# A linear-attention and gated-MLP kernel: chunks 0 and 1 get a triangular solve of their own, and the solve of chunks 2 and 3 goes to GpSimd

## The chip, the core and the metric

The kernel runs on one core of a Trainium2 chip. The core has five engines that run their own instruction lists in order and wait for each other by semaphores: TensorE (PE), VectorE (DVE), ScalarE (ACT), GpSimd (POOL) and SyncE (SP), which here issues the DMA transfers. The metric is the device time of one execution in microseconds, here the median of three runs.

## What is computed

A delta-rule attention over 768 steps for 4 x 8 heads of width 48, and on its output a gated MLP of 3072 tokens, 384 by 1536:

```python
k_n = k / (np.linalg.norm(k, axis=-1, keepdims=True) + 1e-06)
for t in range(S):
    y[:, :, t] = np.einsum('bhd,bhde->bhe', q[:, :, t], state)
    v_old = np.einsum('bhde,bhd->bhe', state, kt)
    state = state + bt[:, :, :, None] * np.einsum('bhd,bhe->bhde', kt, vt - v_old)
x = attn_out.transpose(0, 2, 1, 3).reshape(B * S, H * D)
a = x @ w_a
b = x @ w_b
return (a * b @ w_out)
```

## The kernel before

The 768 steps are cut into 24 chunks of 32. Within a chunk the recurrence is a unit triangular system per head: its 32 x 32 matrix comes from products of keys (the "G" products, TensorE, from the loaded tile `rawb` into a PSUM bank or `duo`), is scaled by VectorE into `b_0`, transposed into `b_1`, and inverted by forward substitution. Chunks go in groups of four (`GROUPS`); one group's 4 x 32 heads fill the 128 partitions, so a group is solved at once. `prep(g)` loads keys, norms and scaling factors and forms the matrices, `solve(g)` inverts, `steps(g)` runs the chunks: state read ("K"), correction ("U"), output ("A"), state update ("S").

The first group is solved in halves (`HALVES`): two 16 x 16 blocks are inverted by 30 dependent VectorE instructions (15 multiplies into `tmp`, 15 subtractions from `b_2`), and `join` builds the missing block on TensorE: the "W" products (64x16 for chunks 0 and 1, 32x16 for 2 and 3), a ScalarE copy `wr`, then the "X" products with the transposed inverse `b_3` and with `xn`. Chunks 0 and 1 use masked, doubled operands (`kk2`, `cx`, `at2`, `tt2`, all lying in the weight tile `wt`), so that a chunk is 16 products of 64x48 instead of 32.

The expert weights come as 12 blocks of 1.15 MB. VectorE decodes each by a TENSOR_SCALAR and two SCALAR_TENSOR_TENSOR instructions over 128x1152 integers. For the first two pairs of chunks the MLP runs in float32 (per block six products with `xb` of 256 columns, a ScalarE copy `a`, a VectorE product `g`, two products of 384 columns), later with float16 parts.

Nothing of the order is written out: every call is put down as an `Op` of the planner class `Plan`, with a price (`price`), the ops it depends on and, for TensorE, a due time (`slot`, `when`). `pack` plays the engines forward and at each step gives a free engine its most urgent ready op; the resulting lists are what the chip runs. While TensorE would idle before 40 us of the plan, `pack` puts in fillers: products of constants into a spare bank (`wide`, `ones`), so that the clock stays up. The plan is made before anything runs: if an engine is slower on the chip than its price, the order stays and the others wait.

Loads are issued by SP in the order of `EARLY`; some are held behind a tiny copy that GpSimd makes once an earlier tile is there:

```python
if over and what != "s" and len(over) < THROTTLE:
    dst = goal(c, what)
    G.tensor_copy(dst, over[max(0, len(over) - 2)])
```

Each such 1x1 copy waits for the load before last and writes into the next load's target, which makes that load wait in turn. The first of them follow chunk 1's correction `u`.

Of the kernel before, what the change touches and what calls it, by code (L numbers as in the profile page):

```python
# [12 lines left out]
F32 = mybir.dt.float32  # L13
# [13 lines left out]
P = 128  # L27
KR = 112
GROUPS = [list(range(i, i + 4)) for i in range(0, NCH, 4)]
# [3 lines left out]
HALVES = [1, 0, 0, 0, 0, 0]  # L33
# [16 lines left out]
def slot(c, piece):  # L50
    if piece == "G" and c < 4:
        v = -30 + 0.1 * c
# [17 lines left out]
EARLY = [(0, "k"), (0, "b"), (2, "k"), (0, "r"), (2, "r")], [(0, "m"), (0, "v"), (2, "v"), (0, "w"), (1, "w")], [(2, "w")], [(3, "w"), (4, "w"), (4, "k"), (4, "r"), (5, "w")], [(6, "w"), (6, "k"), (6, "r"), (7, "w"), (4, "v"), (6, "v"), (8, "w")]  # L70
LAG = 2
THROTTLE = 18
PADS, WARM = 40, 4
# [11 lines left out]
class Plan:  # L85
# [93 lines left out]
    def price(eng, name, outs, ins, kw):  # L179
# [27 lines left out]
        if eng == "DVE":  # L207
# [15 lines left out]
            return (66 + n / speed) / 0.96 + extra  # L223
        return 40 + n / 1.2

    def add(self, eng, fn, name, args, kw):
# [20 lines left out]
        else:  # L247
# [4 lines left out]
            if eng == "PE":  # L252
                op.use += dur
# [46 lines left out]
    def stall(self, o, t, pos, edge, come, then):  # L300
# [3 lines left out]
        while end > edge - self.AHEAD:  # L304
            if then is None:
                enter = max(t + halt + max(0, edge - self.AHEAD - pos) * each, come)
                busy = max(0.0, min(self.BUSY, self.dma - enter - 1000.0)) if enter < 110e3 else 0.0
# [6 lines left out]
        return halt, end, edge, come, then  # L314

    def pack(self, pri, back=False):
# [9 lines left out]
        until, use, warm = self.OPEN, 0.0, True  # L326
# [8 lines left out]
        while len(done) < n:  # L335
# [66 lines left out]
            if e == "PE" and not back:  # L402

                if kept and t > self.SINCE:
# [4 lines left out]
                    def spend(f, many, words, brief):  # L409
                        nonlocal until, warm, use, pos, edge, come, then  # L410
                        while True:
                            while until <= f:
                                warm = use > 0.43 * self.WINDOW if warm else use > 0.75 * self.WINDOW
                                use, until = 0.0, until + self.WINDOW
                            idle.words, idle.dur = words, brief if warm or wide else 2 * brief
# [4 lines left out]
                            use, f = use + idle.dur, f + step[0] + idle.dur  # L420
                            pos, edge, come, then = step[1:]

                    if wide:
                        kept_ = until, warm, use, pos, edge, come, then
                        many = spend(f, 0, 4, 871.0)
                        until, warm, use, pos, edge, come, then = kept_
                        burn = max(0, (edge - self.PEEK - pos - 4 * many) // 4)
                        if burn < 40:
# [5 lines left out]
                        many = spend(f, 0, 4, 871.0)  # L434
                        fine = int((stop_ - f - 871.0 * many) // 218.0)
                        pos += 2 * fine
                    else:
                        many, fine = 0, spend(f, 0, 2, 218.0)
                    fill[i] = burn, many, fine
                while until <= t:  # L440
                    warm = use > 0.43 * self.WINDOW if warm else use > 0.75 * self.WINDOW
                    use, until = 0.0, until + self.WINDOW
# [3 lines left out]
                full = took * o.use / o.dur  # L446
                part = min(1.0, (until - t) / took)
                use += full * part
                if part < 1.0:
                    warm = use > 0.43 * self.WINDOW if warm else use > 0.75 * self.WINDOW  # L450
                    use, until = full * (1 - part), until + self.WINDOW
# [28 lines left out]
    BLOCK, EDGE, FETCH, BUSY, FIRST, AHEAD, STALL, PEEK = 256, 193, 4100.0, 2500.0, 1000.0, 30, 250.0, 2  # L480
# [5 lines left out]
    WINDOW, OPEN = 3413.0, 9800.0  # L486
# [62 lines left out]
def tile_kernel(ctx, tc, kqt, kqs, kn, vn, beta, w, masks, picks, out):  # L549
# [234 lines left out]
    dcs = {}  # L784
    nmr = ring(cst, "nm", 3, [P, 32], F32)
# [9 lines left out]
    tmpt = one("tmp", [P, 256])  # L795
# [60 lines left out]
    def prep(g):  # L856
        chs = GROUPS[g]
        ss = sst
        for c in chs[::2]:
            if g > 1:  # L860
                load(c, "t")
# [6 lines left out]
        s0, s1 = s0t, s1t  # L868
        dc = dcs[g] = dcr()
        nm = nmr()  # L870
# [8 lines left out]
        V.tensor_mul(dc, s0, bt[:, g * 32 : g * 32 + 32])  # L879
# [4 lines left out]
        for ci, c in enumerate(chs[::2] if g > 1 else ()):  # L884
# [28 lines left out]
        for ci, c in enumerate(() if g > 1 else chs):  # L913
            rw = raw(c)
            ga = (duo[:, ci % 2] if g or ci < 1 else att()).rearrange("p (q n) -> p q n", n=64)
            plan.behind = set(ready + hold if g else ())
# [11 lines left out]
            if c == 2:  # L928
                gate.append(len(plan.ops) - 1)
            V.tensor_mul(  # L930
                gnat.rearrange("p k u -> p u k")[:, ci * 8 : ci * 8 + 8, :],
                ga[:, :, 0:32],
# [7 lines left out]
            elif HALVES[g]:  # L940
                kks[c] = ttr()
                plan.behind = {said}
                A.copy(kks[c], ga[:, :, 0:32])
            if ci % 2 == 0:
                at = atr()
            if c < 2:
# [6 lines left out]
                )  # L953
                yield
                continue
            ats[c] = at[:, ci % 2]
            if g < 1:
                plan.behind = {said}
                A.copy(ats[c], ga[:, :, 32:64])
            V.tensor_mul(ats[c], ats[c] if g < 1 else ga[:, :, 32:64], amask.unsqueeze(1).broadcast_to([P, 8, 32]))  # L960
            if c == 3:
                gx = att().rearrange("p (q n) -> p q n", n=64)
                plan.due = slot(c, "G") + 20e3
                with plan.group():
                    for q, h4, a, _ in heads():
                        T.matmul(
                            gx[tok(h4), q, :],
                            raw(0)[feat(h4), a, h4 % 2],
                            raw(1)[feat(h4), a],
                            start=True,  # L970
                            stop=True,
                            skip_group_check=True,
                        )
                for x, h4 in product(range(2), range(4)):
                    o = 32 * ((h4 + x) % 2)
                    A.copy(cx[x][tok(h4), :, o : o + 32], gx[tok(h4), :, o : o + 32])
# [3 lines left out]
        for ci, c in enumerate(chs):  # L980
            (V if g < 1 else G).tensor_mul(
# [6 lines left out]
    def solve(g):  # L988
# [8 lines left out]
        V.tensor_copy(X.rearrange("p t s -> p (t s)")[:, 0 : 33 * 31 + 1 : 33], dtt)  # L997
        size = 16 if HALVES[g] else 32
# [7 lines left out]
        for k in range(size - 1):  # L1006
            m, w = size - 1 - k, k + 1
            tv = tmpt[:, 0 : nb * m * w].rearrange("p (b m w) -> p b m w", b=nb, w=w)
# [368 lines left out]
    st = [lab(f"steps{g}", steps(g, GROUPS[g] if g else [0, 1])) for g in range(NG)]  # L1377
    rest = lab("rest", steps(0, GROUPS[0][2:]))

    plan.stream = "load"  # L1380
    for n, part in enumerate(EARLY[:3]):
        if n == 1:
            G.tensor_copy(mk[0:1, 0:1], rawp(2)[0:1, 0, 0:1])
        if n == 2:
            G.tensor_copy(place(2)[0:1, 0:1], place(0)[0:1, 0:1])
# [11 lines left out]
    for c, what in EARLY[3]:  # L1397
        load(c, what)
# [15 lines left out]
    def opening():  # L1414
# [4 lines left out]
        for c, what in EARLY[4]:  # L1419
            load(c, what)  # L1420
        plan.stream = "rest"
        yield next(pr[1])
        for n in range(2):
            for _ in range(3):
                yield next(rest)
            yield next(pr[1])
            yield next(pr[1])
        yield from chain([rest, pr[1]])
# [9 lines left out]
    merge((moes, 15), (sv[1], 8))  # L1438
# [94 lines left out]
```

## Time and profile before

| | before |
|---|---|
| median of 3 runs (lowest to highest) | 613.67 us (612.68 to 613.83) |
| profiled execution | 613.47 us |
| its span, first to last instruction | 611.7 us |
| PE busy | 601.5 us, 98% |
| DVE busy | 404.1 us, 66% |
| ACT busy | 301.5 us, 49% |
| POOL busy | 34.8 us, 6% |
| mean granted TensorE clock | 0.989 |

Busy time of PE is modelled up to the end of a product's pipeline and includes the fillers; the list of waits tells better where it stood still. In rows of a timeline, several like instructions are merged (x32), and a float32 product leaves two records. The bracket at the end of a row is the idle time of that engine just before it and what ended it.

### The profile page before, as it was taken

Reading aid. Unit: us, or ns where it says so; the run is one execution under the profiler, and the core shown is the slowest. Engines: PE = TensorE matmul, PEld = TensorE weight load, DVE = VectorE, ACT = ScalarE, POOL = GpSimd, SP = SyncE. Lnnn points to the kernel's source line nnn. Section 1 sums busy time; section 2 is a strip of 40 time slices with the busy share of each in tenths; the row PEclk is TensorE's granted clock in tenths of the full one; section 3 lists DMA queues with packets and bytes.
Section 4 is the critical chain, followed back from the end, with each engine's and each line's share of the span. In section 5 each row is a group of like instructions: output and inputs, shape, how many; then the busy total and the mean of one; then the engine's idle time right before and its main releaser. Section 6 shows DMA issues by size and latency. Waiting matters only on the chain.

```text
span 611.7 us, 25252 instructions
## 1 busy us (share of the span) xinstructions
PE 601.5 (98%) x11469; PEld 470.4 (77%) x11469; DVE 404.1 (66%) x1093; ACT 301.5 (49%) x756; POOL 34.8 (6%) x49
## 2 busy tenths in 40 slices
PE   8999999999999999999999999999999999999997
PEld 5588766787778787887787788787777788777875
DVE  5849878897799845699653996553996344244222
ACT  4312313589745753554655366445356445535322
POOL 1000240001100010000101000101000000000000
PEclk9969999999999999999999999999999999999999
DMA  6718688101311204104013013010000000000000
GB/s 221 269 55 318 240 318 301 54 0 32 124 42 48 94 4 153 59 15 135 4 59 122 4 36 115 3 37 20 3 28 3 3 28 2 3 27 3 27 1 26
DMA packets 11931, 46.46 MB, mean 76 GB/s; under 512 B 1328, under 2 KB 4784, under 8 KB 8752
## 3 DMA queue, kind: packets, MB, share of 16 engines
q1 hardware_dynamic: 11824, 44.85, 20.9%
q8 instruction: 89, 1.46, 1.0%
q14 instruction: 18, 0.15, 0.1%
HBM read 40.13 MB, written 4.72 MB: 73 GB/s over the span
## 4 chain that ended last, share of the span: by engine, by line
PE 70%; DVE 5%; ACT 2%; issue 0%
PE bank L545 58%; PE duo L545 9%; PE S_ps L545 2%; DVE b L545 1%; DVE tmp L545 1%; ACT y L545 1%; DVE g L545 1%; DVE wt L545 0%; DVE ghl L545 0%; ACT sqf L545 0%; ACT a L545 0%; DVE at L545 0%; ACT wt L545 0%; DVE f L545 0%; ACT tt L545 0%
## 5 line engine op out<-in xcount | busy, mean ns | idle before, releaser
L545 PE MATMUL bank<-xb,wt 128*128 128x256 f16 (+1 forms) x1800 | 248.5, 291 | 2.4 <-issue 2.4
L545 PEld LDWEIGHTS <-wt 128*128 128x128 f16 x2160 | 208.2, 98 | 35.4 <-issue 0.5
L545 DVE TENSOR_TENSOR g<-bank,a 128x256 f32<-128x256 f32 x144 | 60.4, 419 | 123.4 <-ACT a L545 121.9
L545 PE MATMUL bank<-wt,ghl 128*128 128x384 f16 x720 | 137.1, 326 | 0.0
L545 ACT ACTIVATE a<-bank,gs 128x256 f32<-128x256 f32 x120 | 56.8, 473 | 121.8 <-PE bank L545 121.5
L545 PEld LDWEIGHTS <-ghl 128*128 128x128 f16 x720 | 67.5, 98 | 34.4
L545 PE MATMUL bank<-stage,wt 128*128 128x256 f16 x648 | 76.9, 273 | 0.0
L545 ACT CAST ghl<-g 128x256 f16<-128x256 f32 x120 | 48.4, 403 | 52.1 <-DVE g L545 51.8
L545 DVE TENSOR_TENSOR ghl<-g,ghl 128x256 f16<-128x256 f32 x120 | 51.0, 425 | 34.2 <-ACT ghl L545 33.7
L545 PEld LDWEIGHTS bank<-xb,wt 128*128 128x128 f32 x288 | 53.3, 190 | 14.3 <-issue 3.4
L545 DVE TENSOR_TENSOR b<-b,tmp 128x31 f32<-128x31 f32 (+20 forms) x170 | 56.6, 333 | 3.7
L545 DVE TENSOR_TENSOR tmp<-b,b 128x31 f32<-128x31 f32 (+20 forms) x170 | 56.3, 331 | 3.6
L545 ACT COPY y<-duo 32x384 f32<-32x384 f32 x88 | 41.4, 470 | 3.3 <-PE duo L545 2.2
L545 PE MATMUL bank<-wt,g 128*128 128x384 f32 x96 | 37.3, 500 | 0.0
L545 POOL TENSOR_TENSOR vnb<-vnb,nm 128x384 f32<-128x384 f32 x20 | 18.0, 921 | 128.0 <-DMA vnb<-in_vn 70.2
L545 DVE TENSOR_TENSOR f<-vnb,duo 128x768 f32<-128x768 f32 (+1 forms) x23 | 21.4, 929 | 5.4 <-issue 4.3
L545 ACT COPY a<-bank 128x256 f32<-128x256 f32 x24 | 8.8, 367 | 29.5 <-PE bank L545 29.4
L545 ACT COPY u<-duo 128x768 f32<-128x768 f32 (+1 forms) x23 | 18.0, 784 | 10.2 <-PE duo L545 9.9
L545 ACT ACTIVATE sqy<-y 128x96 f32<-128x96 f32 x80 | 22.3, 278 | 0.9
L545 PEld LDWEIGHTS duo<-sh,rawb 48*64 48x64 f32 x1152 | 18.4, 134 | 4.7 <-issue 2.9
L545 PEld LDWEIGHTS duo<-f,tt 32*32 32x32 f32 x1408 | 16.5, 105 | 6.9 <-issue 4.3
L545 PEld LDWEIGHTS bank<-wt,g 128*128 128x128 f32 x96 | 17.1, 189 | 6.0
(156 smaller groups left out, 624.7 us busy)
## 6 DMA issues: line engine op xcount, KB each, us to landing
rawb<-in_kqt SPq DMA_DIRECT2D x10, 1024.0 KB, 5.0
stage<-in_w SPq DMA_DIRECT2D x6, 1152.0 KB, 6.7
vnb<-in_vn SPq DMA_DIRECT2D x12, 384.0 KB, 4.5
out<-ob SPq DMA_DIRECT2D x24, 192.0 KB, 1.9
knb<-in_kn SPq DMA_DIRECT2D x10, 384.0 KB, 3.5
stage<-in_kqs SPq DMA_DIRECT2D x8, 448.0 KB, 3.9
late<-in_w SPq DMA_DIRECT2D x3, 1152.0 KB, 7.4
wt<-in_w SPq DMA_DIRECT2D x3, 1152.0 KB, 8.4
```

The lines of the kernel that those rows point to most:

```text
L545: fn(*(self.place(a, lease) for a in args), **{k: self.place(a, lease) for k, a in kw.items()})
```

## The change

`GROUPS` becomes [0, 1], [2, 3] and then fours. The first solve therefore has only chunks 0 and 1; it runs the same 30 instructions, with half the partitions unused (zeroed at the start by GpSimd). Its preparation needs one `knb` and one `rawb` load, and the load list puts the second pair's loads behind these. Chunks 2 and 3 become group 1: their G products are made early and copied to SBUF by ScalarE, their scaling and transposition are VectorE's, and their 30 solve instructions are GpSimd's (`E = G if g == 1`), with a `tmp` half of their own. The scaling of V for chunks 0 and 1 moves from two VectorE instructions to 16 ScalarE instructions. Weight blocks 1 and 2 are each held by a 1x1 GpSimd copy behind the solutions `tt2` of chunk 0 and of chunk 1. In the planner, TensorE's activity is kept as a sum of weighted columns, fillers are added where the sum would fall under `NEED`, the price of a GpSimd tensor instruction is 120 + 4.0 n, and the 40 tiny products at the start go. The core of the diff:

```diff
-GROUPS = [list(range(i, i + 4)) for i in range(0, NCH, 4)]
+GROUPS = [[0, 1], [2, 3]] + [list(range(i, i + 4)) for i in range(4, NCH, 4)]
-HALVES = [1, 0, 0, 0, 0, 0]
+HALVES = [int(c[0] < 4) for c in GROUPS]
...
-        v = -30 + 0.1 * c
+        v = -30 + 0.1 * c if c < 2 else -10 + 0.1 * c
...
-        v = 5.0 + 2.2 * (c - 4) if c < 8 else finish(c // 4 * 4 - 4 + c % 4 // 2) - 0.5 + 0.1 * (c % 2)
+        v = 6.5 + 2.2 * (c - 4) if c < 8 else finish(c // 4 * 4 - 4 + c % 4 // 2) - 0.5 + 0.1 * (c % 2)
...
-EARLY = [(0, "k"), (0, "b"), (2, "k"), (0, "r"), (2, "r")], [(0, "m"), (0, "v"), (2, "v"), (0, "w"), (1, "w")], [(2, "w")], ...
+EARLY = [(0, "k"), (0, "b"), (0, "r"), (2, "k"), (2, "r")], [(0, "m"), (0, "v"), (2, "v"), (0, "w")], ...
+SHARE, QUOTA = {32: 0.24, 48: 0.19, 64: 0.5}, 1515.0
-PADS, WARM = 40, 4
+PADS, WARM = 0, 4
...
+        if name.startswith("tensor_") and n > 1:
+            return 120 + 4.0 * n
         return 40 + n / 1.2
...
+                    while t > self.SINCE + self.WINDOW and self.worth(spent, t + o.dur) + o.use < self.NEED:
+                        idle.words, idle.dur = 2, 218.0
+                        halt, pos, edge, come, then = self.stall(idle, t, pos, edge, come, then)
+                        spent.append((t + halt, 218.0, 0.159))
+                        t, fine = t + halt + 218.0, fine + 1
...
-            if c == 2:
-                gate.append(len(plan.ops) - 1)
+            if 1 < c < 4:
+                kks[c] = ttr()
+                A.copy(kks[c], ga[:, :, 0:32])
...
-            (V if g < 1 else G).tensor_mul(
+            if c < 2:
+                for q in range(8):
+                    x = vnc(c)[:, q * D : q * D + D]
+                    A.activation(x, x, AF.Copy, scale=nm[:, ci * 8 + q : ci * 8 + q + 1])
+                continue
+            (V if c < 4 else G).tensor_mul(
...
+        E = G if g == 1 else V
...
-            V.tensor_mul(tv, lk.unsqueeze(3).broadcast_to([P, nb, m, w]), xk.broadcast_to([P, nb, m, w]))
+            E.tensor_mul(tv, lk.unsqueeze(3).broadcast_to([P, nb, m, w]), xk.broadcast_to([P, nb, m, w]))
             xs = blocks(X, k + 1, m, 0, w)
-            V.tensor_sub(xs, xs, tv)
+            E.tensor_sub(xs, xs, tv)
...
+    for _ in range(4):
+        next(st[0])
+    plan.stream = "load"
+    G.tensor_copy(place(1)[0:1, 0:1], tt2[0][0:1, 0, 0:1])
+    hold[:] = [len(plan.ops) - 1]
+    load(1, "w")
+    G.tensor_copy(place(2)[0:1, 0:1], tt2[1][0:1, 0, 0:1])
+    hold[:] = [len(plan.ops) - 1]
+    load(2, "w")
+    hold.clear()
+    run_all(st[0])
     for b in range(1, 3):
         run_all(ws[b])
-    run_all(st[0])
+    run_all(pr[1])
+    run_all(sv[1])
```

How the instructions move is seen best in three places. On VectorE, behind the first solve, before (`f_71` is chunk 1's correction, `xb` the token block for the MLP, `late` and `stage` are raw weight blocks):

```order
L545 STREAM_TRANSPOSE xn<-b_2_69 128x512
L545 TENSOR_TENSOR vnb<-vnb,nm_138 128x384 x2
L545 TENSOR_TENSOR wt<-bank_61,mk 128x512
L545 TENSOR_TENSOR wt<-at_75,mk 128x512 x2
L545 TENSOR_SCALAR wt<-late 128x1152
L545 TENSOR_TENSOR f_71<-vnb,duo 128x384
L545 TENSOR_TENSOR wt<-bank_63,mk 128x512
L545 SCALAR_TENSOR_TENSOR wt<-late,wt 128x1152
L545 STREAM_TRANSPOSE xb<-y_89 128x384
```

and now:

```order
L559 TENSOR_TENSOR f_71<-vnb,duo 128x384
L559 RECIPROCAL s_133<-s_134 128x16
L559 TENSOR_TENSOR dc_137<-s_133,bt 128x16
L559 TENSOR_TENSOR wt<-bank_62,mk 128x512
L559 TENSOR_TENSOR b_0_67<-tt_79,dc_137 128x8x32
L559 TENSOR_TENSOR b_0_67<-tt_80,dc_137 128x8x32
L559 STREAM_TRANSPOSE dt<-dc_137 128x32
L559 STREAM_TRANSPOSE b_1_68<-b_0_67 128x1024
L559 COPY b_2_69<-dt 128x32
L559 SCALAR_TENSOR_TENSOR wt<-late,wt 128x1152
L559 STREAM_TRANSPOSE xb<-y_89 128x384
```

The two V scalings are gone from here, and the second group's scaling and transposition (`dc_137` to `b_2_69`) stand between chunk 1's solution (`wt<-bank_62`) and the first weight block's decode.

On GpSimd, from chunk 1's correction `u_72` on, before:

```order
L545 COPY wt<-u_72 1x1 x2
L545 COPY knb<-wt 1x1
L545 COPY rawb<-wt 1x1
L545 COPY wt<-knb 1x1
L545 COPY late<-rawb 1x1
```

and now the middle of the solve behind it (`b_1_68` the matrices, `b_2_69` the growing inverse):

```order
L559 TENSOR_TENSOR tmp<-b_1_68,b_2_69 128x120
L559 TENSOR_TENSOR b_2_69<-b_2_69,tmp 128x2x10x6
L559 COPY knb<-wt 1x1
L559 TENSOR_TENSOR tmp<-b_1_68,b_2_69 128x126
L559 TENSOR_TENSOR b_2_69<-b_2_69,tmp 128x2x9x7
L559 TENSOR_TENSOR tmp<-b_1_68,b_2_69 128x128
L559 TENSOR_TENSOR b_2_69<-b_2_69,tmp 128x2x8x8
L559 TENSOR_TENSOR tmp<-b_1_68,b_2_69 128x126
L559 COPY rawb<-wt 1x1
```

The copies that hold later loads now stand among the solve's instructions, the first behind the twelfth, and each solve instruction waits for the one before it.

On TensorE, from the first expert product (`bank<-xb,wt`) to chunk 2's W products (`b_3_70,tt_79`), before:

```order
L545 MATMUL bank_63<-xb,wt 128x256 x6
L545 MATMUL S_ps<-wt,knb 48x48 x32
L545 MATMUL S_ps<-u_72,knb 48x48 x32
L545 MATMUL bank_61<-xb,wt 128x256 x6
L545 MATMUL bank_62<-xb,wt 128x256 x6
L545 MATMUL bank_64<-b_3_70,tt_79 32x16 x32
```

and the end of that stretch now:

```order
L559 MATMUL bank_63<-xb,wt 128x256 x6
L559 MATMUL bank_64<-wt,g_97 128x384
L559 MATMUL bank_62<-wt,g_97 128x384
L559 MATMUL bank_61<-xb,wt 128x256 x6
L559 MATMUL bank_64<-wt,g_98 128x384
L559 MATMUL duo<-sh_73,rawb 64x48 x32
L559 MATMUL bank_62<-wt,g_98 128x384
L559 MATMUL bank_63<-b_3_70,tt_79 32x16 x32
```

Chunk 2's W products stood behind the products of three weight blocks; now they stand behind those of four and behind the outputs of the first two. On VectorE the transposition that makes their `b_3_70` out of GpSimd's `b_2_69` now stands behind the decode of block 4 and the fourth `g`.

## Rows read from the trace of the kernel before

**Rows 1.** The page's head and its busy time of TensorE.

```profile
span 611.7 us, 25252 instructions
PE 601.5 (98%) x11469; PEld 470.4 (77%) x11469; DVE 404.1 (66%) x1093; ACT 301.5 (49%) x756; POOL 34.8 (6%) x49
```

**Rows 2.** Whom TensorE waited for, from 44.7 to 150 us (first two rows) and from 150 us on (last row): total us, times, longest.

```profile
PE bank L545 <- issue: 2.4, 3, 1.3
PE duo L545 <- issue: 0.6, 1, 0.6
...
PE duo L545 <- DVE at L545: 0.3, 1, 0.3
```

**Rows 3.** Busy us of each engine in stretches of 5 us, then the granted TensorE clock (PEclk), the DMA share and GB/s.

```profile
35.00:40.00 5.00, 5.00 (x128) 4.22 (x126) 2.67 (x4) 0.48 (x1) 0.00 (x0) 0.50 0.02 3
40.00:45.00 5.00, 4.99 (x90) 4.09 (x87) 3.23 (x5) 1.70 (x3) 0.91 (x2) 0.76 0.35 88
50.00:55.00 5.00, 5.00 (x82) 4.18 (x83) 5.00 (x7) 0.82 (x4) 0.58 (x2) 1.00 0.72 209
```

**Rows 4.** The opening in order of time: start us, duration us, engine, line, operation, out<-in, count.

```profile
3.78 0.84 ACT L545 ACTIVATE sqf<-knb 128x768 f32<-128x768 f32 x1 [1.55 <-DMA knb<-in_kn]
...
7.19 0.84 ACT L545 ACTIVATE sqf<-knb 128x768 f32<-128x768 f32 x1 [2.57 <-DMA knb<-in_kn]
...
9.64 1.10 PE L545 MATMUL duo<-rawb 48*32 48x64 f32 x64 [0.74 <-DMA rawb<-in_kqt]
...
12.31 1.83 PEld L545 LDWEIGHTS bank<-rawb 48*32 48x32 f32 x128 [0.42 <-DMA rawb<-in_kqt]
...
13.48 0.61 DVE L545 TENSOR_TENSOR b<-bank,dc 128x256 f32<-128x256 f32 x1 [0.86 <-PE bank L545]
...
15.01 1.25 DVE L545 STREAM_TRANSPOSE b<-b 128x1024 f32<-128x1024 f32 x1
...
16.29 0.19 DVE L545 TENSOR_TENSOR tmp<-b,b 128x30 f32<-128x30 f32 x1
...
24.95 1.31 DVE L545 STREAM_TRANSPOSE b<-b 128x512 f32<-128x512 f32 x2
...
26.17 1.02 DVE L545 STREAM_TRANSPOSE xn<-b 128x512 f32<-128x512 f32 x1
...
28.84 0.69 DVE L545 TENSOR_TENSOR wt<-bank,mk 128x512 f32<-128x512 f32 x1 [0.74 <-issue]
...
44.10 0.58 DVE L545 STREAM_TRANSPOSE xb<-y 128x384 f32<-128x384 f32 x1 [1.77 <-ACT y L545]
...
44.74 0.48 PE L545 MATMUL bank<-xb,wt 128*128 128x256 f32 x1
```

**Rows 5.** Loads of weights and products on TensorE in the opening, same columns; the first two rows are two dense records at the start, the third the fillers of the first solve.

```profile
4.95 0.34 PEld L545 LDWEIGHTS bank<-ones 128*128 128x128 f32 x1 [0.52 <-issue]
5.80 0.34 PEld L545 LDWEIGHTS bank<-ones 128*128 128x128 f32 x1 [0.52 <-issue]
...
17.40 7.99 PE L536 MATMUL bank<-ones 128*128 128x512 f32 x18
...
28.65 1.73 PE L545 MATMUL bank<-b,wt 64*64 64x16 f32 x29
...
37.34 1.94 PE L545 MATMUL bank<-wt 64*64 64x48 f32 x32
...
42.45 1.10 PE L545 MATMUL bank<-u,wt 64*64 64x48 f32 x32
```

**Rows 6.** Three ScalarE entries of the opening, same columns.

```profile
9.05 0.23 ACT L545 ACTIVATE s<-ss 128x32 f32<-128x32 f32 x1 [1.02 <-DVE ss L545]
...
12.20 1.49 ACT L545 COPY wt<-duo 32x256 f32<-32x256 f32 x4 [2.92 <-DVE b L545]
...
17.06 2.99 ACT L545 COPY wt<-bank 32x256 f32<-32x256 f32 x8
```

**Rows 7.** GpSimd in order of time, same columns.

```profile
56.92 0.18 POOL L545 COPY late<-rawb 1x1 f32<-1x1 f32 x1 [3.75 <-DMA rawb<-in_kqt]
...
64.62 1.16 POOL L545 COPY rawb<-late 1x1 f32<-1x1 f32 x1 [2.67 <-DMA late<-in_w]
...
76.08 1.28 POOL L545 COPY stage<-vnb 1x1 f32<-1x1 f32 x1
77.41 1.61 POOL L545 TENSOR_TENSOR vnb<-vnb,nm 128x384 f32<-128x384 f32 x2
```

**Rows 8.** VectorE in order of time, same columns: a decode's first step, and what ran at the moments of rows 7.

```profile
41.58 0.75 DVE L545 TENSOR_SCALAR wt<-stage 128x1152 int32<-128x1152 int32 x1
...
56.92 0.95 DVE L545 TENSOR_TENSOR f<-vnb,duo 128x768 f32<-128x768 f32 x1
...
64.39 2.82 DVE L545 SCALAR_TENSOR_TENSOR wt<-wt 128x1152 int32<-128x1152 int32 x2
...
75.97 1.36 DVE L545 SCALAR_TENSOR_TENSOR wt<-stage,wt 128x1152 int32<-128x1152 int32 x1
...
78.01 2.23 DVE L545 SCALAR_TENSOR_TENSOR wt<-stage,wt 128x1152 int32<-128x1152 int32 x1
```

**Rows 9.** All two-operand GpSimd instructions of the kernel before, minimum, median and maximum ns.

```profile
L545 POOL TENSOR_TENSOR vnb<-vnb,nm x20: 820/832/1354, 77.4 to 415.3; 128x384 f32<-128x384 f32 x20
```

**Rows 10.** One weight block's six products of 256 columns at full clock, on TensorE.

```profile
131.43 2.75 PE L545 MATMUL bank<-xb,wt 128*128 128x256 f32 x12
```

More of the change, by code (lines that the diff above doesn't have):

```diff
@@ L407, in pack, with spend @@
                     stop_, burn, many = t - (self.SLACK if wide else 150.0), 0, 0
-                    def spend(f, many, words, brief):
-                        nonlocal until, warm, use, pos, edge, come, then
+                    def spend(f, many, words, brief, use):
+                        nonlocal pos, edge, come, then
                         while True:
[L412 to L415, printed above, removed]
+                            idle.words, idle.dur = words, brief
                             step = self.stall(idle, f, pos, edge, come, then)
@@ L445, in pack @@
                 small = o.small
[L446 to L451, printed above, removed]
+                spent.append((t + halt, took, o.use))
+                del spent[:-400]
             else:
@@ L784, in tile_kernel @@
     dcs = {}
+    G.memset(b4.tiles[0].rearrange("p (a b) -> p a b", b=32)[:, :, 16:32], 0.0)
+    for t in dcr.tiles:
+        G.memset(t, 0.0)
     nmr = ring(cst, "nm", 3, [P, 32], F32)
@@ L953, in prep @@
                 )
+                if c == 1:
+                    gx = att().rearrange("p (q n) -> p q n", n=64)
+                    plan.due = slot(c, "G") + 20e3
+                    with plan.group():
+                        for q, h4, a, _ in heads():
+                            T.matmul(
+                                gx[tok(h4), q, :],
+                                raw(0)[feat(h4), a, h4 % 2],
+                                raw(1)[feat(h4), a],
+                                start=True,
+                                stop=True,
+                                skip_group_check=True,
+                            )
+                    for x, h4 in product(range(2), range(4)):
+                        o = 32 * ((h4 + x) % 2)
+                        A.copy(cx[x][tok(h4), :, o : o + 32], gx[tok(h4), :, o : o + 32])
                 yield
@@ L956, in prep @@
             ats[c] = at[:, ci % 2]
-            if g < 1:
-                plan.behind = {said}
+            if c < 4:
                 A.copy(ats[c], ga[:, :, 32:64])
[L960 to L976, printed above, removed]
+            V.tensor_mul(ats[c], ats[c] if c < 4 else ga[:, :, 32:64], amask.unsqueeze(1).broadcast_to([P, 8, 32]))
             yield
@@ L1376, in tile_kernel @@
     sv = [lab(f"solve{g}", solve(g)) for g in range(NG)]
-    st = [lab(f"steps{g}", steps(g, GROUPS[g] if g else [0, 1])) for g in range(NG)]
-    rest = lab("rest", steps(0, GROUPS[0][2:]))
+    st = [lab(f"steps{g}", steps(g, GROUPS[g])) for g in range(NG)]
+    rest = lab("rest", steps(1, GROUPS[1]))
     plan.stream = "load"
-    for n, part in enumerate(EARLY[:3]):
+    for n, part in enumerate(EARLY[:2]):
         if n == 1:
             G.tensor_copy(mk[0:1, 0:1], rawp(2)[0:1, 0, 0:1])
-        if n == 2:
-            G.tensor_copy(place(2)[0:1, 0:1], place(0)[0:1, 0:1])
         hold[:] = [len(plan.ops) - 1] * (n > 0)
@@ L1418, in opening @@
         plan.stream = "load"
-        for c, what in EARLY[4]:
+        for c, what in EARLY[3]:
             load(c, what)
         plan.stream = "rest"
-        yield next(pr[1])
+        yield next(pr[2])
         for n in range(2):
@@ L1425, in opening @@
                 yield next(rest)
-            yield next(pr[1])
-            yield next(pr[1])
-        yield from chain([rest, pr[1]])
+            yield next(pr[2])
+            yield next(pr[2])
+        yield from chain([rest, pr[2]])
     first = opening()
@@ L1441, in tile_kernel @@
     run_all(sp)
-    for g in range(1, NG):
+    for g in range(2, NG):
         n = len(GROUPS[g])
```

77 lines of the change are left out of this document (43 added, 34 removed).

## The prediction

> **What bounds the kernel now.** I read the page's busy times first, then TensorE's waits, then the clock by stretch, then the opening in order of time, last what GpSimd and VectorE do at the same moments. TensorE is busy 601.5 of 611.7 us [rows 1]. The waits say more: from 44.7 us on it waits 2.4 + 0.6 us before 150 us and 0.3 us in all the rest [rows 2]. The first expert product stands at 44.74 us [rows 4]. So behind 44.74 the kernel is one TensorE stream of 567 us, and a change acts in two ways only: it moves the 44.74, or it adds or removes TensorE waits behind it. The profiled execution took 613.47 us (span 611.7 and 1.8 around it), 0.2 below the median, so I sum against 613.47; changes under 0.2% (1.2 us) cannot be told from none.
>
> The opening is a chain: kn(0) and the k/q block land, products, scaling, transposition, 30 dependent VectorE instructions (16.29 to 24.95), two transpositions more, small products of chunks 0 and 1 until 43.6, the transposition at 44.10 [rows 4]. The granted clock is 0.50 from 35 to 40 and 0.76 from 40 to 45 us [rows 3], and one group of 64x48 products takes 1.94 at the half level against 1.10 at full clock [rows 5].
>
> **The change part by part: the opening.** Loads: the first k/q block now goes ahead of kn(2). Before, TensorE takes up the block at 9.64, 2.45 us behind kn(2) at 7.19 [rows 4], for 1024 KB; kn(2)'s 384 KB at that rate are 0.9 us, so 8.7. Bounds: 6.2 (3.78 + 2.45) and 9.6. The diagonal factors need one kn load alone: ScalarE's root came 1.86 us behind the second load's square (7.19 to 9.05 [rows 6]), behind the first that is 5.65, and 3 us of small VectorE instructions still end before the products. A first VectorE read comes 1.17 us after its products start (12.31 to 13.48), the second chunk's 0.9 later: 10.75; its 0.6, the transposition's 1.25 and gaps give a solve start of 12.65 against 16.29, 3.65 us earlier. The solve has the same 30 instructions and sizes (the halved group fills half the partitions), so it keeps its 8.66 us, and the transposition into xn ends at 23.55 instead of 27.2.
>
> V scaling: two VectorE multiplies (0.98 us) leave; 16 ScalarE instructions come. The nearest row is 0.23 us for 128x32 [rows 6], so 3.7 us. ScalarE starts its copies near 10.5, has 7.5 us of them (1.49 for four, 2.99 for eight [rows 6]), then these, then 1.65 us: done near 23.3, just before the first product result at 23.4. I take 0; if one took 0.4, the chain would be 2.7 us late.
>
> Behind xn VectorE now is the longer chain. Two masks of the solution's size, 0.65 each, to 24.85; the first solution at 25.9 (before 1.65 us behind xn, now with three fillers of 0.22) to 26.5; the added reduction and the first decode step to 28.1; six small ones of the second group to 29.6; f at 30.0 if the small products run at full clock; 0.6 more; the second solution at 31.7 to 32.4; the second group's two multiplies, transposition and copies to 35.05; then decode 1.3, x 0.5, decode 1.3 plus a GpSimd turn, x 0.5: the first expert product at 39.1. That is **5.6 us earlier**. If the clock falls as before, five 64x48 groups cost 0.8 us each, chunk 1's 64x16 group (over 1.73 [rows 5]) some 0.7, and the start is near 42.2, 2.5 earlier. The new order puts fillers into the very holes before which the clock fell, so I take full clock and keep 42.2 as a bound. The 40 tiny start products that go (about 1 us of a TensorE that waits for the load anyway) count nothing.
>
> **The change part by part: the solve on GpSimd.** It has 30 instructions of 30 to 128 elements, mean 91, and four 1x1 copies for loads in between. The trace has no such instruction. The nearest rows are a 1x1 copy at 0.175 and a 128x384 multiply at 0.82 [rows 7, 9]; on a line between them 91 elements take 0.32 us, plus a step from one to the next, which I take at 0.1 (TensorE follows VectorE by 0.06 at 44.68 [rows 4]): all 34 alone would need 13.7 us. Started at 35.15, that is 49 us, in time for TensorE.
>
> But they aren't alone. A 1x1 copy took 1.16 us at 64.62 and 1.28 at 76.08, and ended at 65.78 and 77.36, just behind VectorE's decode instructions that end near 65.75 and at 77.33; another, beside a VectorE instruction that reads PSUM and one SBUF operand (56.92), took 0.18 [rows 7, 8]. It works the other way too: the decode instruction at 78.01 took 2.23 instead of 1.36 beside the two GpSimd multiplies that end at 79.02. So whichever runs holds the other off whole, where VectorE reads two SBUF operands or runs the 0.75 us first decode step. And from 35 us on VectorE is full of just these: 10 decode steps of 1.3, four of 0.7 and one 0.5 multiply (16.3 us) against 3.5 us of free kinds (two x transpositions, four g, a reduction) until the transposition that waits for GpSimd. One GpSimd instruction goes between each two; by then the next dependent one is 0.1 late and waits a whole decode step.
> - VectorE reaches that transposition at 35.1 + 19.8 + about 3 of holding (some 10 turns of 0.3) = 57.9. GpSimd has had 15 turns and about 3 in free stretches: 18 of 34. The other 16 run alone at 0.38: 64.0.
> - TensorE: the weights of block 3 are decoded at 52.4 instead of about 49.9; block 3's six products take 2.6 (12 records [rows 10], less overlap), one output product, chunk 2's reading of the state and another output product 2.4: it stands before chunk 2's W products at 57.4. Without holding it would be there at 39.1 + 16.0 = 55.1. W can start at 64.0 + 0.65 + 0.25 = 64.9. Waits: 2.3 + 7.5 = **9.8 us**, at a place where before it waits 0. Later loads hang on the same GpSimd queue, but they are needed after VectorE's own delay, so I add none.
> - After 7.5 idle us the clock may be at half again. At the start dense records follow each other by 0.85 us, later 18 of them take 7.99 [rows 5], so 0 to 3.4 us; I take 1.0.
>
> [...]
>
> **Sum.** 613.47 - 5.6 + 9.8 + 1.0 = 618.7. Bounds: GpSimd at 0.18 with no step ends at 60.9 (615.6), at 0.45 with 0.2 near 67 (621.7); the k/q block -1.4 to +0.9 (the first less where VectorE's other work binds); ScalarE 0 to 2.7; clock 0 to 3.1 in the opening and -1.0 to +2.4 behind the stall. The scaling, the loads' new holds behind the two solutions (weights land some 7 us later, 3 us before VectorE wants them) and the later due time of the chunk 4 to 7 products move nothing that TensorE waits for.
>
> **The rivals.**
> - *GpSimd keeps pace*: its 34 instructions end before TensorE needs them. This needs a mean of 0.57 us each (19.5 us from 35.1 to 54.6); from there on there is no stall. For it: alone they need 0.42; VectorE also waits for products and weights, and each such hole lets GpSimd run on. Against it: VectorE is busy 5.00 of the 5 us from 50 on [rows 3], with the same decode. Time: 613.47 - 5.6 + 0.5 = 608.4, faster. Chance 0.38.
> - *Half a stall*: VectorE's holes let GpSimd take two turns in every second place, the wait shrinks to 4 to 6 us and eats the opening's gain: 612 to 615. Chance 0.15.
> - *The opening stays slow*: ScalarE's 16 instructions or a clock that falls again put the first expert product at 42.2; VectorE's second group then comes 3 us later as well, and the stall stays: 613.47 - 2.5 + 8.8 + 1.0 = 620.8. For it: the clock fell in this stretch before. Against: the fillers. Chance 0.07.
> - *Forecast*, stall behind the shared ports: 0.40, own range 615 to 622.
>
> **How the numbers follow.** Slower: 0.38 of the forecast's 0.40, 0.07, and 0.03 of the half stall: 0.48. Within 0.2%: 0.02 and 0.10, 0.12. Faster: 0.38 and 0.02, 0.40. The range goes from 607 (a third of the first rival lies below) to 621.5 (a tenth above).
>
> **What would show it.** Right: first expert product near 39; GpSimd's small instructions spread over 35 to 64 us with many of 1 us and more; a VectorE transposition that waits for GpSimd near 58 to 64; a TensorE wait of 6 to 9 us ahead of the 32x16 products and a clock below 1.00 just behind. Wrong: GpSimd instructions of 0.2 to 0.6 us ending before 55, no TensorE wait there; or a first expert product later than 42.

## The result, and the profile after

The changed kernel takes 619.03 us (median of 15 executions, 616.89 to 623.97), the kernel before beside it 613.83 (610.56 to 617.45): ratio 1.0092, 95% interval 1.0070 to 1.0115, slower by 0.9%. The profiled execution took 616.89 us, the least of its fifteen, 2.1 under their median. Executions of one kernel differ in the clock that they are granted (means of 0.982 to 0.994 among these fifteen), and the profiled one of x10_decode_due ran at 0.75 throughout (span 747.9 us), so that only the length of GpSimd's solve is read from it.

The page's head, its busy time of TensorE, and TensorE's longest waits behind the first expert product with us in total, times, longest (as [rows 1, 2]):

```profile
span 615.1 us, 25088 instructions
PE 596.2 (97%) x11351; PEld 466.2 (76%) x11351; DVE 408.5 (66%) x1105; ACT 304.8 (50%) x773; POOL 56.7 (9%) x84
...
PE bank L559 <- DVE b L559: 5.0, 1, 5.0
...
PE duo L559 <- DVE f L559: 1.3, 1, 1.3
...
PE S_ps L559 <- ACT u L559: 0.9, 1, 0.9
```

One wait of 5.0 us stands alone, and two of about 1 us that the kernel before has not. The opening in order of time, with the same columns as [rows 4]:

```profile
8.46 1.10 PE L559 MATMUL duo<-rawb 48*32 48x64 f32 x64 [1.32 <-DMA rawb<-in_kqt]
...
12.50 0.19 DVE L559 TENSOR_TENSOR tmp<-b,b 128x30 f32<-128x30 f32 x1
...
17.39 3.72 ACT L559 ACTIVATE vnb<-vnb,nm 128x48 f32<-128x48 f32 x16
...
22.40 1.03 DVE L559 STREAM_TRANSPOSE xn<-b 128x512 f32<-128x512 f32 x1
...
37.47 2.86 PE L559 MATMUL bank<-xb,wt 128*128 128x256 f32 x12 [0.67 <-DVE xb L559]
```

The first expert product stands at 37.47 instead of 44.74. Busy us by stretch in order PE, PEld, DVE, ACT, POOL, then granted clock, DMA share, GB/s (as [rows 3]):

```profile
40.00:45.00 5.00, 4.76 (x119) 3.57 (x120) 5.00 (x6) 1.57 (x3) 4.69 (x5) 1.00 0.49 197
...
55.00:60.00 5.00, 0.29 (x1) 0.00 (x0) 2.82 (x4) 0.00 (x0) 3.89 (x10) 0.71 0.92 336
60.00:65.00 5.00, 4.67 (x72) 3.36 (x73) 5.00 (x8) 0.90 (x2) 2.49 (x4) 0.61 0.68 281
```

The opening now keeps the full clock (1.00 in each 5 us up to 55), where [rows 3] have 0.50 and 0.76; it falls at 55 to 65 us (0.71 and 0.61), around a stretch in which TensorE does nothing. GpSimd's solve, from its first to its last instruction:

```profile
34.03 1.26 POOL L559 TENSOR_TENSOR tmp<-b,b 128x30 f32<-128x30 f32 x1 [0.27 <-DVE b L559]
...
45.97 1.55 POOL L559 TENSOR_TENSOR b<-b,tmp 128x120 f32<-128x120 f32 x1
47.47 0.70 POOL L559 COPY knb<-wt 1x1 f32<-1x1 f32 x1
...
50.12 0.40 POOL L559 TENSOR_TENSOR tmp<-b,b 128x128 f32<-128x128 f32 x1
50.60 0.45 POOL L559 TENSOR_TENSOR b<-b,tmp 128x128 f32<-128x128 f32 x1
...
58.87 0.24 POOL L559 TENSOR_TENSOR tmp<-b,b 128x30 f32<-128x30 f32 x1
59.19 0.25 POOL L559 TENSOR_TENSOR b<-b,tmp 128x30 f32<-128x30 f32 x1
```

One shape, 128x30, takes 1.26 us at 34.03 and 0.24 at 58.87. What stood beside them, on VectorE, ScalarE and TensorE:

```profile
48.05 1.69 DVE L559 SCALAR_TENSOR_TENSOR wt<-wt 128x1152 int32<-128x1152 int32 x1
52.25 0.42 DVE L559 TENSOR_TENSOR g<-bank,a 128x256 f32<-128x256 f32 x1 [2.50 <-ACT a L559]
...
59.47 1.30 DVE L559 STREAM_TRANSPOSE b<-b 128x512 f32<-128x512 f32 x2 [2.18 <-POOL b L559]
...
51.12 0.84 ACT L559 ACTIVATE sqf<-knb 128x768 f32<-128x768 f32 x1 [4.78 <-POOL b L559]
...
60.33 1.05 PE L559 MATMUL bank<-b,tt 32*32 32x16 f32 x64 [5.04 <-DVE b L559]
```

From 49.7 to 52.2 VectorE waits for a copy on ScalarE, which stands behind a square of keys; that waits for a load that GpSimd's queue released late (the copy into knb at 47.47). In just those 2.5 us GpSimd runs at 0.39 to 0.45 per solve instruction, and starts six of its 34 (one of them a copy). At the end VectorE waits 2.18 for GpSimd and TensorE 5.04 for VectorE.

### The profile page after: what moved, and what is told of

Read it like the earlier page. It is cut to its first block, busy times and chain, and to the rows that moved or that the text cites. A ratio compares the mean times of both kernels' runs of the same rounds, so it can differ in the third digit from the quotient of the medians.

```text
span 615.1 us, 25088 instructions
## 1 busy us (share of the span) xinstructions
PE 596.2 (97%) x11351; PEld 466.2 (76%) x11351; DVE 408.5 (66%) x1105; ACT 304.8 (50%) x773; POOL 56.7 (9%) x84
## 4 chain that ended last, share of the span: by engine, by line
PE 83%; DVE 6%; ACT 4%; POOL 4%; issue 1%; DMA 1%; SPq 0%; POOLq 0%; ACTq 0%
PE bank L559 67%; PE duo L559 12%; PE S_ps L559 3%; POOL b L559 2%; DVE b L559 2%; ACT wt L559 2%; POOL tmp L559 2%; DVE wt L559 1%; DMA rawb<-in_kqt 1%; PE bank L550 1%; DVE tmp L559 1%; ACT y L559 1%; DVE g L559 0%; DVE ss L559 0%; ACT tt L559 0%
## 5 line engine op out<-in xcount | busy, mean ns | idle before, releaser
L559 ACT COPY sh<-S_ps 112x768 f32<-112x768 f32 x22 | 17.6, 798 | 13.7 <-PE S_ps L559 13.7
```

Of the source, the lines that this page charges most:

```text
L559: fn(*(self.place(a, lease) for a in args), **{k: self.place(a, lease) for k, a in kw.items()})
```

## The experiments

Theories: **1**, VectorE and GpSimd hold each other off, which stretches the second solve; **2**, GpSimd is that slow by itself; **3**, the load copies in its queue slow it; **4**, the waits at 175 us come from the later due time. One number beside each median comes from the profiled execution: first expert product to the span's end, so without the opening. It is 567.0 us before and 577.6 after.

**x1_decode** (leaves out the unpacking of four weight blocks):

```
-        V.tensor_scalar(d, hi, 5, 2, ...)
-        V.scalar_tensor_tensor(d, hi, -0x40000000, d, ...)
-        V.scalar_tensor_tensor(d, lo, 29, d, ...)
+        if b in range(1, 5):
+            V.tensor_scalar(d, hi, 0x3FFF0000, None, op0=ALU.bitwise_and)
+            for _ in range(2):
+                V.transpose(d.bitcast(F32), d.bitcast(F32))
...
```

The first step becomes a mask of the same size. The other blocks keep their three steps.

> The two SCALAR_TENSOR_TENSOR of the unpacking of weight blocks 1 to 4 are replaced by STREAM_TRANSPOSEs of the same 128x1152, with one operand; the instructions of all engines keep their order. This leaves out the unpacking of those four blocks, nothing else. Theory 1 (VectorE's two-operand steps and GpSimd hold each other off): GpSimd's solve, 25.4 us in the changed kernel, takes 13 to 18 us, its steps of 128x120 about 0.4 us instead of 1.4 to 1.6; TensorE's 5.0 us wait ahead of chunk 2's W products is under 1 us; the granted clock stays near 1 between 55 and 65 us; the time falls by 4 to 7 us, to 612 to 615. Theory 2 (GpSimd is that slow by itself on these shapes) and theory 3 (the small copies on its queue that wait for transfers slow it): the solve stays within 2 us of 25.4, the wait and the time stay as they are, 617 to 621.

Measured: 611.68 us, ratio 0.9959 (0.9926 to 0.9992); 572.4 behind the opening. Its opening ran in part at half clock (0.50 from 30 to 40 us), so the solve starts 7.0 us later and the first expert product 8.0. GpSimd, VectorE and the W products on TensorE:

```profile
41.07 0.23 POOL L559 TENSOR_TENSOR tmp<-b,b 128x30 f32<-128x30 f32 x1
41.37 1.34 POOL L559 TENSOR_TENSOR b<-b,tmp 128x30 f32<-128x30 f32 x1
...
49.44 0.45 POOL L559 TENSOR_TENSOR b<-b,tmp 128x128 f32<-128x128 f32 x1
...
54.32 0.72 POOL L559 TENSOR_TENSOR tmp<-b,b 128x78 f32<-128x78 f32 x1
...
57.77 0.53 POOL L559 TENSOR_TENSOR b<-b,tmp 128x30 f32<-128x30 f32 x1
...
41.27 1.32 DVE L559 SCALAR_TENSOR_TENSOR wt<-late,wt 128x1152 int32<-128x1152 int32 x1
...
49.13 1.35 DVE L559 STREAM_TRANSPOSE wt<-wt 128x1152 f32<-128x1152 f32 x1
...
54.02 0.84 DVE L559 TENSOR_SCALAR wt<-wt 128x1152 int32<-128x1152 int32 x1
...
61.98 0.74 PE L559 MATMUL bank<-b,tt 32*32 32x16 f32 x64
...
63.58 2.76 PE L559 MATMUL bank<-wt,g 128*128 128x384 f32 x8
```

The solve takes 17.2 us (41.07 to 58.30) with VectorE as busy as before. Instructions beside transpositions take 0.45 and less; long ones are left beside the one two-operand step still there (1.34 at 41.37) and beside the TENSOR_SCALAR steps (0.72 at 54.32), and a shorter one beside the multiply of vnb and nm on VectorE (0.53 at 57.77, where the changed kernel's took 0.25 at 59.19 with VectorE waiting). TensorE's wait is under 1 us, the clock is 1.00 from 50 to 70, and the time is 7.35 us under the changed kernel's, a little more than expected, and 0.4% under the kernel before's. Theory 1 holds; 2 and 3 fall, since shapes, copies and order are the same. Against 3 speaks the changed kernel's own trace, too: GpSimd has no idle time ahead of any copy of the solve, and the four take 0.70, 0.17, 0.17 and 0.17.

**x2_vsolve**, the second solve back on VectorE (`E = G if g == 1 else V` becomes `E = V`):

> The second solve goes back to VectorE, all else as in the changed kernel. Theory 1: the 30 steps of 0.2 to 0.4 us run there in 8 to 10 us, unpacking is as fast as before the change, and chunk 2's W products come without a wait over 2 us: 612 to 617. Rival (VectorE has no room for 10 us more in the first 25 us of expert work, so that the unpacking and the gates come late and the expert products wait): waits of TensorE for wt or g that sum to over 5 us between 37 and 75 us, 618 to 624.

621.33 us, ratio 1.0104 (1.0061 to 1.0147); 580.5 behind the opening. TensorE's waits:

```profile
PE duo L559 <- issue: 4.6, 2, 3.5
...
PE S_ps L559 <- issue: 2.2, 1, 2.2
PE bank L559 <- issue: 1.1, 2, 0.7
```

The time is the rival's, its reason is not: waits for wt or g stay under 0.5 us, and 7.9 us are waits for no engine, mostly between 75 and 94 us. The other plan of the whole kernel undoes what is compared, so this run says nothing on what GpSimd's share is worth; with the order kept, that was not tried.

**x3_price** (`return 120 + 4.0 * n` becomes `return 700.0 if n < 200 else 900.0`):

> The planner's price of a tensor operation on GpSimd is raised from 160 to 630 ns to the measured 700 to 900 ns, so that it sets other work of TensorE ahead of chunk 2's W products. Theory 1 with the wait as the main loss: the 5.0 us wait goes to under 1.5 us, the clock stays near 1 between 55 and 65 us, and the time falls by 4 to 7 us, to 612 to 615, with the waits of 175 to 184 us unchanged or up to 2 us longer. Rival (the lost time only moves, since chunks 2 to 7 then come later and expert blocks run out in the same way): the wait is gone but waits of the same sum stand between 65 and 190 us, 617 to 621.

624.04 us, ratio 1.0160 (1.0124 to 1.0196); 584.9 behind the opening.

```profile
PE bank L559 <- DVE wt L559: 5.4, 3, 4.7
PE duo L559 <- issue: 2.8, 1, 2.8
```

The rival holds in part: the wait for the solution is gone, and 4.7 us for a weight block that VectorE now unpacks late stand in its place, with half clock behind (0.50 from 65 to 70). But this wait ends at 65 us, ahead of the stretch that the rival named, and the time is 3 us above its range.

**x4_due** (`v = 6.5 + 2.2 * (c - 4)` becomes `v = 5.0 + ...`):

> The due time of the G products of chunks 4 to 7 goes back from 6.5 to 5.0. Theory 4 (this due time makes the chain of chunks 4 to 7 late, and that is the 3.4 us of waits at 175 to 184 us): those waits fall under 1 us and the time falls by 2 to 4 us, to 615 to 617, while the 5.0 us wait at 60 us stays. Rival (the late solve makes that chain late, not the due time): the waits at 175 to 184 us stay, and the time is within 1.5 us of 619.

617.78 us, ratio 1.0064 (1.0036 to 1.0092); 575.9 behind the opening. TensorE's waits from 150 to 200 us, first the changed kernel's, then this one's:

```profile
PE duo L559 <- DVE f L559: 1.3, 1, 1.3
PE S_ps L559 <- ACT u L559: 0.9, 1, 0.9
PE bank L559 <- DVE n L559: 0.6, 2, 0.5
```

```profile
PE bank L559 <- DVE n L559: 0.9, 1, 0.9
PE S_ps L559 <- ACT u L559: 0.2, 1, 0.2
```

The waits are 1.7 us fewer, as theory 4 has it, and x1_decode shows that they don't come from the late solve: there chunk 2's W products stand 16.6 us behind the first expert product instead of 22.9, and these waits are the same 1.3 and 0.9. Behind them the changed kernel's clock falls once more:

```profile
180.00:185.00 5.00, 4.82 (x145) 4.36 (x146) 4.22 (x15) 3.20 (x7) 0.00 (x0) 0.66 0.03 7
...
181.64 1.50 PE L559 MATMUL duo<-u,at 32*32 32x48 f32 x64
```

In x4_due, whose clock is 1.00 from 150 to 200, the same products take 0.88 (at 187.15). With the group ahead of them (starts at 180.19 and at 186.29) the difference is 1.2 us. But in x4_due waits of 1.4 on issue and 1.3 for g come at 70 to 94 us; the median is 1.25 us lower, less than the two intervals can tell apart, and above the 615 to 617 of theory 4.

**x7_split**, order kept (a half's fixed price in the planner is halved to that end):

```
+        n = 2 if b in range(1, 5) else 1
+        parts = [slice(i * WD // n, (i + 1) * WD // n) for i in range(n)]
...
+            for r in parts:
+                V.scalar_tensor_tensor(d[:, r], lo[:, r], 29, d[:, r], ...)
```

> Each of the three unpacking steps of weight blocks 1 to 4 is cut into two instructions of 128x576, all engines keep their order. Theory 1 (GpSimd gets its turn between two VectorE instructions, so that what counts is how long one VectorE instruction is): GpSimd's solve falls from 25.4 us to between 17 and 21, since its stretched steps wait some 0.6 us less each; TensorE's wait ahead of chunk 2's W products falls from 5.0 us to between 0.5 and 3; the time to between 613 and 617, though VectorE pays about 0.8 us for twelve more starts. Rival (what holds GpSimd is VectorE's total traffic, which stays): the solve stays within 1.5 us of 25.4 and the time at 618 to 621.

615.92 us, ratio 1.0045 (1.0015 to 1.0075); 577.3 behind the opening. GpSimd and TensorE's waits:

```profile
42.67 0.82 POOL L559 TENSOR_TENSOR b<-b,tmp 128x120 f32<-128x120 f32 x1
...
57.47 0.25 POOL L559 TENSOR_TENSOR b<-b,tmp 128x30 f32<-128x30 f32 x1
...
PE bank L559 <- DVE wt L559: 2.5, 3, 1.3
...
PE bank L559 <- DVE b L559: 1.2, 1, 1.2
```

The turn is right: the 128x120 step takes 0.82 instead of 1.55. The solve is not: 23.25 us from 34.47, where 17 to 21 were expected, and VectorE no longer has its 2.5 us hole (it is busy 5.00 of 5 us from 35 to 60), so that most instructions wait their turn until 57 us. The wait for the solution falls to 1.2, and waits for unpacked weights take 2.5. Behind the opening the profiled executions differ by only 0.3 us; the medians differ by 3.1. How much the cut gives stays open. The 0.8 us for twelve more starts is an estimate that the trace of the kernel before bears out: from one VectorE start to the next a 128x256 product takes 0.33 (at 49.05) and a 128x768 one 0.86 (at 56.92), so on a line 0.065 for the start and 0.8 for twelve; no figure of x7_split shows it.

**x8_split_due**, both edits:

> The cut of x7_split together with the due time 5.0 of x4_due. If the two losses are separate, the gains add: 1 to 2 us under x7_split, 611.5 to 615.5, with no wait over 1 us at 170 to 190 us. Rival (they are one loss: an earlier solve makes the chain of chunks 4 to 7 early anyway, or the other due time only moves its waits to 70 to 100 us): within 0.8 us of x7_split, or above it.

616.33 us, ratio 1.0048 (1.0022 to 1.0074): the gains don't add. The waits at 175 us are gone, and 1.2 on issue and 1.4 for g stand at 82 to 94.

**x10_decode_due**, x1_decode and x4_due together (leaves out the unpacking of four weight blocks):

> The one-operand unpacking of x1_decode (which leaves out the unpacking of weight blocks 1 to 4) with the due time 5.0 of x4_due. If the first loss (VectorE against GpSimd) and the second (the due time) are two separate ones, the gains add: 1 to 3.5 us under x1_decode's 611.7, that is 608 to 610.7, with a GpSimd solve of 14 to 18 us, a wait under 1 us ahead of chunk 2's W products and none over 1 us at 170 to 190 us. Rival (they don't add, since what the other due time saves at 175 us it gives back at 70 to 105 us): 611 to 613.

611.79 us, ratio 0.9964 (0.9940 to 0.9987), the same as x1_decode: the rival. The solve took 16.5 us (36.44 to 52.92), as expected, though at that clock VectorE has holes of up to 1.1 us that help it. So in these two pairs the due time is worth nothing that lasts; in x8_split_due the waits only stand elsewhere.

**x6_need0** (`NEED = 1.12` becomes `0.0`):

> The planner's bound NEED goes from 1.12 to 0, so that it sets no filler products ahead of a product to keep the clock; all else as in the changed kernel. If those fillers are what keeps the clock at full speed in the opening: the granted clock is near 0.5 in at least 5 us between 20 and 45 us, the first expert product is 2 to 6 us later than 37.5, and the time is 620 to 625. Rival (the shorter opening keeps the clock by itself, and the fillers only take TensorE's time): the clock stays near 1 until 55 us, the first expert product comes within 0.5 us of 37.5, and the time is 617 to 619.5.

627.42 us, ratio 1.0234 (1.0186 to 1.0281); first expert product 38.9; 584.4 behind the opening.

```profile
105.00:110.00 5.00, 3.56 (x89) 2.91 (x78) 2.10 (x5) 0.18 (x1) 0.17 (x1) 0.78 0.68 193
```

Neither: the opening loses 1.4 us, at a clock of 0.75 from 20 to 25, and the time is above both ranges. The largest losses lie at 100 to 125 us, with waits of 2.1 for g and 1.4 on issue and a clock of 0.78 to 0.88, where the changed kernel has 1.00 throughout. The fillers, with the order that comes of them, are worth 8 us, but mostly not in the opening; what part is the clock and what the other order, this run can't say.

**x9_vscale**, the eight-fold `A.activation(x, x, AF.Copy, scale=...)` of chunks 0 and 1 taken out, so that VectorE scales:

> The scaling of V of chunks 0 and 1 goes from ScalarE (16 activations, 3.7 us) back to VectorE (two TENSOR_TENSOR). If VectorE's chain sets the opening, as the prediction has it, the first expert product is 0.5 to 1.5 us later than 37.5 and the time 0 to 1.5 us longer, 619 to 621. Rival (ScalarE's chain sets it there): the first expert product is 0.5 us or more earlier, 616.5 to 618.5.

622.15 us, ratio 1.0130 (1.0092 to 1.0168); first expert product 40.2. Inconclusive: the time is above both ranges, its clock was 0.85 and 0.81 from 15 to 25 us, and kernels with the opening of the changed one came as late under such a clock (below).

**x11_prices** and **x12_prices_due**, the cut of x7_split with measured prices (`700.0` for a GpSimd step, `860.0` and `580.0` for the halves), without and with the due time 5.0:

> The cut unpacking of x7_split, with the planner told the measured durations of both sides: 700 ns for each GpSimd step, 860 and 580 ns for the halves on VectorE that run beside it. If wrong prices are why TensorE waits at 40 to 65 us, its waits for wt and b there sum to under 1.5 us (3.7 in x7_split) and the time is 611 to 614.5. Rival (the prices are not the point: each new order of TensorE's work meets other waits for its instructions and another clock, as x2_vsolve and x3_price did): the waits for wt and b are gone, but 3 us or more of waits on issue and of half clock stand between 60 and 120 us, and the time is 616 to 623.

> x11_prices with the due time 5.0. As x8_split_due was to x7_split: no waits over 1 us at 170 to 190 us, and the time within 1.5 us of x11_prices, under it if waits on issue between 60 and 120 us don't grow. A time under 613 would beat both kernels.

617.89 us, ratio 1.0071 (1.0046 to 1.0095), and 615.30, ratio 1.0015 (0.9989 to 1.0041). The longest waits of the first, then of the second:

```profile
PE bank L561 <- DVE g L561: 6.1, 3, 3.0
```

```profile
PE S_ps L561 <- issue: 2.8, 1, 2.8
```

In x11_prices the waits for wt and b are gone (0.9 us in all), and 6.1 us for g come in their place, where the rival had named issue: VectorE is the short side there (busy 5.00 of 5 us in seven of the eight stretches from 35 to 75). x12_prices_due, 2.6 us lower where at most 1.5 were expected, is the best complete kernel tried and can't be told from the kernel before.

**x13_fill**, fillers in the gap, into the bank that is overwritten next:

```
+                if i == self.mark:
...
+                    for _ in range(21):
+                        self.nc.tensor.matmul(bank, x, x.unsqueeze(1).broadcast_to([P, 4, P]), ...)
```

> The changed kernel with 21 filler products (128x512, 0.22 us each at the full clock, 4.6 us in all) ahead of chunk 2's W products, into the bank that these then overwrite, so that they run in the 5.0 us in which TensorE waits there; the other instructions keep their order. If that wait is what halves the clock from 57.5 to 63.9 us, the granted clock stays near 1 between 55 and 65 us, GpSimd's solve and the first work after it stay where they are, and the time falls by 1 to 1.8 us, to 617.2 to 618. Rival (the small products that follow, or the machine, set the clock there, not the wait): the clock is still under 0.75 in one of the two windows and the time is 619 to 620.5.

622.59 us, ratio 1.0161 (1.0133 to 1.0189); 579.7 behind the opening.

```profile
15.00:20.00 5.00, 3.12 (x70) 2.38 (x70) 4.45 (x17) 4.92 (x19) 0.00 (x0) 0.71 0.92 319
20.00:25.00 5.00, 5.00 (x8) 1.98 (x7) 4.76 (x12) 2.84 (x10) 0.95 (x1) 0.61 0.10 41
55.00:60.00 5.00, 5.00 (x81) 3.18 (x81) 3.96 (x5) 1.38 (x3) 4.68 (x9) 1.00 0.76 269
60.00:65.00 5.00, 4.79 (x82) 2.48 (x81) 3.29 (x6) 0.28 (x1) 2.48 (x10) 1.00 0.93 344
```

The theory holds for the clock: with the gap filled (the W products start at 63.58) it is 1.00 from 55 to 70. It fails for the time, which is above both ranges: a wait of 2.5 on issue came at 75 us, and the opening had a clock of 0.71 and 0.61 from 15 to 25, so that the first expert product stood at 41.0.

## Why the prediction came out as it did

The direction was right, and that the stall comes of VectorE and GpSimd holding each other off is what x1_decode shows: with transpositions in place of the unpacking's two-operand steps, the solve takes 17.2 us instead of 25.4 and the wait of 5.0 is under 1. The forecast's line puts it down to shared ports; no trace or run shows ports, only these lengths. That 618.7 came within 0.4 us of 619.03 is luck: with what they measured in the profiled executions, the forecast's own terms give 613.47 - 7.27 + 5.55 + 1.2 = 613.0, no slowdown at all. The other 3.9 us of the 616.9 come from what the prediction put at nothing or did not have, and why the median lies 2.1 above that is not shown.

- **Opening, -5.6**: -7.27 in the profiled execution. The loads (8.46 against 8.7), the solve's start (12.50 against 12.65), the transposition into xn (ending 23.43 against 23.55) and the scaling (3.72 against 3.7, hidden) came as worked out. What failed is the chain behind xn: the second group's preparation was done at 33.95, not 35.05, and the first product came 3.5 behind it, not 4.05. The bound of 42.2 carries over 3.1 of the 4.7 us that it lists, and doesn't say what hides the rest.
- **GpSimd alone, 13.7**: its free steps sum to about 13 (0.24 at 30 elements, 0.40 to 0.45 at 128, 0.08 from one to the next).
- **GpSimd beside VectorE, 28.9**: 25.4. One turn per held step is what x1_decode (1.34 beside a two-operand step, 0.45 and less beside transpositions) and x7_split (0.82 beside half steps, 1.55 beside whole ones) show; what failed is the count of turns. "18 of 34" were to be done before VectorE's transposition; when VectorE began to wait for it, at 57.29, it was 27. Six of them started in the hole of 2.5 us, which the prediction did not have: it gave the later loads on GpSimd's queue no price ("I add none"), and one of these, into knb, held ScalarE's square, and VectorE with it.
- **TensorE's waits, 2.3 + 7.5**: 0.55 + 5.0. The stall is mis-sized by a third, since GpSimd ended at 59.4, not 64.0, while TensorE stood there at 55.3, not 57.4. By its size the rival of half a stall (4 to 6 us) came true, and by its reason, VectorE's holes, in part; its time, 612 to 615, did not. The delay of 2.3 by late weights hardly came: 0.24 and 0.31.
- **Clock, +1.0**: 1.2. Chunk 2's W products, one product of 128x256 and four output products run from 60.33 to 65.79 (where the X products start), 5.46 us; in x1_decode at full clock from 61.98 to 66.27, 4.3.
- **"The later due time ... move nothing"**: wrong. TensorE's waits between 120 and 200 us sum to 3.4, against 0.3 before, and the clock behind them costs the 1.2 shown under x4_due. That x4_due takes most of them away, with the solve as late as before, shows whose they are. What the due time is worth in the end depends on the rest of the order: x4_due, x8_split_due, x10_decode_due and x12_prices_due stand -1.25, +0.4, +0.1 and -2.6 us from the kernels that they alter, and only of the last pair do the intervals lie apart.

Sum in the profiled executions: 613.47 - 7.27 + 10.7 = 616.9. Of the 10.7 behind the opening, waits are 6.9 (10.2 against 3.3), the clock 1.2 behind the stall and 1.2 at 180 us; 1.4 are in pieces that I did not tie to a cause. The median lies 2.1 above that execution; openings that lose the clock, as in the last section, would do that, but no profile of such an execution of the changed kernel itself was taken.

Where the opening's gain went is shown for the largest part: x1_decode alone takes off 7 us. Even then only 2 of the 7.27 us remain against the kernel before. Where the other 5 went stays open: the trace of x1_decode has the waits at 175 us and a clock of 0.50 and 0.82 from 180 to 190, but x10_decode_due, with the other due time, was no faster.

## What to carry to other kernels

Before a chain of small dependent instructions goes to GpSimd, look at what VectorE runs at that time, not at how busy it is: beside transpositions the chain kept its pace (0.45 us and less per instruction in x1_decode), beside integer unpacking of two operands most of its instructions waited up to a whole step (ten took 1.26 to 1.62 us in the changed kernel, beside steps of 1.32 to 1.69). Undo one suspect with the order of all engines kept (x1_decode, x7_split); edits that let the planner choose anew moved the time by up to 8 us, for reasons that could be told only in part.

## What was not expected of the hardware

- VectorE's TENSOR_SCALAR on 128x1152 integers holds GpSimd off too (0.72 us for a step of 0.32, at 54.32 in x1_decode), as the prediction took it to. Its rows don't have that, but the trace of the kernel before does, where a 1x1 copy ends with such a step:

```profile
75.27 0.70 POOL L545 COPY vnb<-stage 1x1 f32<-1x1 f32 x1 [3.21 <-DMA stage<-in_w]
...
75.18 0.76 DVE L545 TENSOR_SCALAR wt<-stage 128x1152 int32<-128x1152 int32 x1 [0.22 <-DMA stage<-in_w]
```

  That a transposition of the same size does not (0.45 at 49.44), no row before had shown.
- One opening, kernels that share its order: first expert product at 37.5 (changed kernel), 37.9 (x4_due, x7_split), 39.6 (x8_split_due), 41.0 (x13_fill) and 45.4 us (x1_decode). The granted clock parts them: 1.00 from 15 to 25 us in the first three, 0.90 and 0.76 in the fourth, 0.71 and 0.61 in the fifth; in x1_decode 0.73 from 10 to 15 and half level from 30 to 40. A gain in such a stretch is not the same in each execution.
- In the fourth and fifth the fillers themselves hold up the work. VectorE's first solve starts at 13.10 and 12.96 there, against 12.50, but the filler products ahead of the first W products take longer, first the changed kernel's, then those of x13_fill:

```profile
17.80 3.70 PE L550 MATMUL bank<-ones 128*128 128x512 f32 x8
...
19.15 6.04 PE L550 MATMUL bank<-ones 128*128 128x512 f32 x8
```

  The first W products start at 22.03 in the changed kernel and at 25.55 in x13_fill. So fillers that were set for the full clock took 2.3 us more (6.04 against 3.70) ahead of TensorE's own work when the clock fell to 0.71 and 0.61 in spite of them.
- TensorE waited up to 3.5 us for no engine at 70 to 110 us, at other places in each order (2.5 at 75 in x13_fill, where 42 instructions more stood ahead). What it waits for there, these profiles don't name.
